# Fewer, larger weight transfers at the end of a decode kernel: A_wo in two transfers instead of four, B_w_down in four instead of five

## The chip, the cores and the metric

One core of one Trainium2 chip. The time is device microseconds (us) of a whole execution, the median of several; a fast run is one not slowed by a lower clock. The kernel before takes 81.61 us. The profile is one execution; its span, 79.8 us, is a little shorter than the timed execution.

In the profile, PE is the matrix engine (PEld its weight loads), DVE the vector engine, ACT the scalar engine, and SP the engine whose queue (SPq) issues the bulk transfers. A line of a timeline gives start and duration in us; `[0.49 <-DMA ...]` says that the engine had been idle for 0.49 us and that this transfer's landing ended the wait.

## The reference, cut to what matters

One token (512 values) goes through a layer norm, then through two branches that are added: attention with a window of 4096 cached keys and values (8 KV heads, 32 query heads of 128), closed by `@ wo`, and a gated MLP closed by `@ w_down`.

```
x  = A_x;  xn = layernorm(x)
a  = softmax(q @ k.T * 128**-0.5) @ v          # k, v: last 4096 rows of the caches, 8 heads
a  = a.reshape(1, 4096) @ wo                   # wo:     4096 x 512 bf16, 4.2 MB
y  = (silu(xn @ w_gate) * (xn @ w_up)) @ w_down   # w_down: 1792 x 512 bf16, 1.8 MB
out = x + a + xn + y * sigmoid(xn @ w_r)       # one token, so the routing picks it
```

With a single token every weight and every cached row is read once: 30.7 MB.

## The kernel before

All bulk loads are issued on the SP queue in the order in which they are used: wq, k, v, gate, up, wo, w_down. A_wo and w_down go to where the keys were, so their issue waits until the sixth head's keys have been copied away. In memory each of 128 partitions holds 32 consecutive rows of A_wo (32 KB) and 14 of w_down (14 KB). A transfer of 8 rows of A_wo is therefore 128 pieces of 8 KB.

```python
    def fill(n):                       # matmuls on zeros: keep TensorE's clock up
        for _ in range(2 * n):
            te.matmul(ps[:, 7, :], lhsT=zst[:], rhs=zmov[:], start=True, stop=True)
    # ... (scores, softmax, values, gate and up are cut) ...
    SP.need((s_c[1], 6))
    wo_v = A_wo.rearrange("(p j) n -> p (j n)", j=RJ)
    wo_chunks = [(0, 8), (8, 16), (16, 24), (24, 32)]
    t_wo = [dma(sy, f"wo{k}", wo_sb[:, j0 * D:j1 * D], wo_v[:, j0 * D:j1 * D]) for k, (j0, j1) in enumerate(wo_chunks)]
    wd_v = B_w_down.rearrange("(p j) n -> p (j n)", j=FB)
    wd_chunks = [(0, 4), (4, 8), (8, 11), (11, 13), (13, 14)]
    t_wd = [dma(sy, f"wd{k}", wd_sb[:, j0 * D:j1 * D], wd_v[:, j0 * D:j1 * D]) for k, (j0, j1) in enumerate(wd_chunks)]
    # ... cut ...
    for k, (j0, j1) in enumerate(wo_chunks):
        PE.need(t_wo[k])
        for j in range(j0, j1):
            ins = grouped(j, oT2[:, j:j + 1], wo_sb)      # one 1x512 matmul
        if k in (1, 2):
            with te.Fori(0, 3):
                fill(1)
    t_g4 = PE.mark(ins)
    DVE.need(t_g4, t_rf)
    fill(1)
    t_part = DVE.mark(ve.tensor_tensor(out=part, in0=a_ps, in1=rf, op=ALU.add))
    PE.need(t_hT)
    for k, (j0, j1) in enumerate(wd_chunks):
        PE.need(t_wd[k])
        for j in range(j0, j1):
            ins = by_halves(hTr[:, j, 0:1], wd_sb[:, j * D:(j + 1) * D], stop=(j == FB - 1))   # two 1x256 matmuls
        if k == 0:
            PE.need(t_part, t_sel4)
            by_halves(sel4[:], part)
    # ... two copies and the store of the result
```

Of the kernel before, what the change touches and what calls it, by code (L numbers as in the profile page):

```python
# [38 lines left out]
def kernel(  # L39
# [112 lines left out]
    te, ac, ve, gp, sy = nc.tensor, nc.scalar, nc.vector, nc.gpsimd, nc.sync  # L152

    def fill(n):
        for _ in range(2 * n):
            te.matmul(ps[:, 7, :], lhsT=zst[:], rhs=zmov[:], start=True, stop=True)  # L156

    def dma(eng, name, out_, in_):
        s = S("d_" + name)
        eng.dma_start(out=out_, in_=in_).then_inc(s, 16)  # L160
        return (s, 16)
# [192 lines left out]

    SP.need((s_c[1], 6))
    wo_v = A_wo.rearrange("(p j) n -> p (j n)", j=RJ)
    wo_chunks = [(0, 8), (8, 16), (16, 24), (24, 32)]
    t_wo = [dma(sy, f"wo{k}", wo_sb[:, j0 * D:j1 * D], wo_v[:, j0 * D:j1 * D]) for k, (j0, j1) in enumerate(wo_chunks)]
    wd_v = B_w_down.rearrange("(p j) n -> p (j n)", j=FB)
    wd_chunks = [(0, 4), (4, 8), (8, 11), (11, 13), (13, 14)]  # L360
    t_wd = [dma(sy, f"wd{k}", wd_sb[:, j0 * D:j1 * D], wd_v[:, j0 * D:j1 * D]) for k, (j0, j1) in enumerate(wd_chunks)]

    POOL.need((pe_t, 4 * HKV))
# [131 lines left out]
    def grouped(j, lhsT, w):  # L495
        c = j % 4
        return te.matmul(a_ps[32 * c:32 * c + 1, :], lhsT=lhsT, rhs=w[:, j * D:(j + 1) * D], start=False, stop=False,
                         tile_position=(0, 32 * c), skip_group_check=True)
# [7 lines left out]
    for k, (j0, j1) in enumerate(wo_chunks):  # L506
        PE.need(t_wo[k])
        for j in range(j0, j1):
            ins = grouped(j, oT2[:, j:j + 1], wo_sb)
        if k in (1, 2):  # L510
            with te.Fori(0, 3):
                fill(1)
    t_g4 = PE.mark(ins)
    DVE.need(t_g4, t_rf)
    fill(1)
    t_part = DVE.mark(ve.tensor_tensor(out=part, in0=a_ps, in1=rf, op=ALU.add))
    PE.need(t_hT)
    for k, (j0, j1) in enumerate(wd_chunks):
# [44 lines left out]
```

## Time and profile before

| | before |
|---|---|
| time, median of the first 3 runs | 81.61 us (81.58 to 81.94) |
| span of the profiled execution | 79.8 us |
| HBM read | 30.67 MB |
| last w_down transfer: middle part in / last part in | 75.31 / 76.82 us |

The DMA part of the page of before. Columns of the queue lines: packets, megabytes, and the time of their packets as a share of sixteen engines' span.

```profile
DMA packets 3178, 30.72 MB, mean 385 GB/s; under 512 B 356, under 2 KB 487, under 8 KB 999
...
q1 hardware_dynamic: 3170, 30.67, 91.9%
q8 instruction: 2, 0.03, 0.2%
q14 instruction: 2, 0.01, 0.0%
```

A packet is here one contiguous piece of one partition; the 356 smallest are mostly the writes to semaphores. The queues 8 and 14 are fetches of the program itself.

Two things that no view prints singly are used below: the trace's records of each packet (start, size, duration) and of each of the sixteen parts in which a transfer lands. Where they are quoted, it is as plain tables.

### The profile page before, as it was taken

How to read it: one execution, taken by the hardware profiler on the slowest of the kernel's cores; microseconds unless marked ns; L12 is line 12 of the kernel's file. 1: busy time of each engine (PE TensorE's matmuls, PEld its weight loads, DVE VectorE, ACT ScalarE, POOL GpSimd, SP SyncE). 2: the span in 40 equal slices, each digit the busy share in tenths (PEclk: the TensorE clock that was granted, in tenths of full speed). 3: DMA queues.
4: the chain of work that ended last, by engine and by line, in shares of the span. 5: the costliest groups of instructions: out<-in, count | busy, mean ns of one | idle time of the engine just before them, and what ended most of it. 6: DMA issues, size and time to landing. Idle time of an engine off the chain costs nothing.

```text
span 79.8 us, 1627 instructions
## 1 busy us (share of the span) xinstructions
PE 58.1 (73%) x634; PEld 30.3 (38%) x636; DVE 44.1 (55%) x96; ACT 30.4 (38%) x41; POOL 10.2 (13%) x22
## 2 busy tenths in 40 slices
PE   0010873849998997997996696778887799996750
PEld 0010401236875865865864224222232254231310
DVE  3778100166538769669693652988889348303020
ACT  1941000502379689589568026232233420000010
POOL 5930000000102202202205900000000000000000
PEclk9999999999999999999999999999999999999996
DMA  1899999999999999999999999999999999999600
GB/s 25 271 469 419 394 444 407 423 444 444 460 403 419 460 427 403 419 476 419 394 423 468 411 403 435 431 420 410 453 439 378 427 419 423 423 392 405 215 6 1
DMA packets 3178, 30.72 MB, mean 385 GB/s; under 512 B 356, under 2 KB 487, under 8 KB 999
## 3 DMA queue, kind: packets, MB, share of 16 engines
q1 hardware_dynamic: 3170, 30.67, 91.9%
q8 instruction: 2, 0.03, 0.2%
q14 instruction: 2, 0.01, 0.0%
q10 hardware_dynamic: 4, 0.00, 0.0%
HBM read 30.67 MB, written 0.00 MB: 385 GB/s over the span
## 4 chain that ended last, share of the span: by engine, by line
DMA 44%; SPq 22%; PE 18%; ACT 6%; DVE 4%; issue 2%
DMA k_sb<-in_B_w_down_dram 30%; SPq L160 22%; DMA wq_sb<-in_A_wq_dram 15%; PE ps L328 11%; ACT kT L303 6%; PE ps L337 3%; PE ps L256 2%; DVE kin L295 2%; PE ps L268 1%; DVE kT L300 1%; PE ps L502 1%; DVE qpad L273 1%; DVE kT L528 1%; SPq L558 0%; SPq L74 0%
## 5 line engine op out<-in xcount | busy, mean ns | idle before, releaser
L303 ACT COPY kT<-ps 128x1024 bf16<-128x1024 bf16 x19 | 18.6, 1015 | 9.6 <-PE ps L328 9.6
L328 PE MATMUL ps<-perm_bf,kin 128*128 128x128 bf16 x256 | 19.3, 235 | 1.2 <-DVE kin L295 0.9
L328 PEld LDWEIGHTS ps<-perm_bf,kin 128*128 128x128 bf16 x256 | 16.4, 106 | 5.7 <-issue 4.4
L295 DVE COPY kin<-k_sb 128x2048 bf16<-128x2048 bf16 x16 | 10.9, 686 | 3.1 <-PE ps L328 3.1
L300 DVE COPY kT<-ps 128x1024 bf16<-128x1024 bf16 x13 | 9.0, 691 | 4.1 <-PE ps L328 3.5
L423 ACT CAST pvS<-ps 128x512 bf16<-128x512 f32 x8 | 4.7, 585 | 10.0 <-PE ps L429 10.0
L337 PE MATMUL ps<-kT,qAB 128*32 128x512 bf16 x68 | 7.2, 414 | 1.7 <-ACT kT L303 1.7
L288 POOL COPY qAB<-qpad 128x64 bf16<-128x64 bf16 x8 | 3.5, 444 | 34.0 <-PE ps L337 34.0
L156 PE MATMUL ps<-zmov,zst 128*128 128x512 bf16 x25 | 6.6, 381 | 0.2 <-issue 0.2
L403 DVE COPY vin<-v_sb 128x2048 bf16<-128x2048 bf16 x8 | 5.5, 685 | 1.1 <-PE ps L438 0.9
L409 DVE COPY vin<-v_sb 128x2048 bf16<-128x2048 bf16 x8 | 5.5, 682 | 0.0
L438 PE MATMUL ps<-vin,pTcur 128*32 128x512 bf16 x32 | 3.2, 386 | 2.6 <-ACT pvS L423 2.2
L256 PE MATMUL ps<-wq_sb,xnT 128*1 128x512 bf16 x32 | 3.8, 621 | 1.7 <-DMA wq_sb<-in_A_wq_dram 1.7
L450 PE MATMUL ps<-zmov,zst 128*128 128x512 bf16 x16 | 4.7, 376 | 0.0
L529 ACT CAST kT<-ps 1x256 bf16<-1x256 f32 x1 | 0.4, 362 | 11.4 <-PE ps L502 11.4
L273 DVE COPY qpad<-ps 128x16 bf16<-128x16 bf16 x4 | 0.5, 170 | 7.5 <-PE ps L268 7.5
L212 PE MATMUL ps<-ident_bf,xn_row 1*128 1x1 bf16 x4 | 0.3, 166 | 4.8 <-POOL qAB L189 4.8
L262 ACT CAST q<-ps 128x512 bf16<-128x512 f32 x2 | 1.2, 585 | 6.6 <-PE ps L256 6.6
L444 PE MATMUL ps<-vin,pTcur 128*32 128x512 bf16 x32 | 3.2, 387 | 0.3 <-DVE vin L409 0.2
L337 PEld LDWEIGHTS ps<-kT,qAB 128*32 128x32 bf16 x68 | 1.9, 93 | 3.9 <-issue 1.7
L438 PEld LDWEIGHTS ps<-vin,pTcur 128*32 128x32 bf16 x32 | 1.1, 92 | 6.0 <-DVE vin L403 5.5
L156 PEld LDWEIGHTS ps<-zmov,zst 128*128 128x128 bf16 x26 | 2.0, 97 | 3.2 <-issue 1.7
(95 smaller groups left out, 54.2 us busy)
## 6 DMA issues: line engine op xcount, KB each, us to landing
v_sb<-in_A_v_cache_dram SPq DMA_DIRECT2D x4, 2048.0 KB, 39.7
k_sb<-in_A_k_cache_dram SPq DMA_DIRECT2D x3, 2048.0 KB, 24.1
wq_sb<-in_A_wq_dram SPq DMA_DIRECT2D x2, 2048.0 KB, 9.5
k_sb<-in_A_wo_dram SPq DMA_DIRECT2D x4, 1024.0 KB, 32.8
k_sb<-in_A_k_cache_dram SPq DMA_DIRECT2D x2, 1024.0 KB, 14.7
wq_sb<-in_B_w_gate_dram SPq DMA_DIRECT2D x1, 1792.0 KB, 42.9
wq_sb<-in_B_w_up_dram SPq DMA_DIRECT2D x1, 1792.0 KB, 46.9
k_sb<-in_B_w_down_dram SPq DMA_DIRECT2D x2, 512.0 KB, 33.8
```

Source lines behind the costliest of these rows:

```text
L156: te.matmul(ps[:, 7, :], lhsT=zst[:], rhs=zmov[:], start=True, stop=True)
L160: eng.dma_start(out=out_, in_=in_).then_inc(s, 16)
L256: ins = te.matmul(ps[32 * c:32 * c + 1, hf, :], lhsT=xnT[:, kt:kt + 1], rhs=wq_sb[:, kt, (4 * hf + c) * 512:(4 * hf + c + 1) * 512], start ...
L295: ve.tensor_copy(out=kin[:, 2 * h:2 * h + 2, :], in_=k_sb[:, g, 2 * h:2 * h + 2, :]).then_inc(s_c[h], 1)
L300: ve.tensor_copy(out=kT[:, b, :], in_=tp[:, b, :]).then_inc(s_ev[b], 1)
L303: ac.copy(out=kT[:, b, :], in_=tp[:, b, :]).then_inc(s_ev[b], 1)
L328: ins = te.transpose(tp[:, b, k * P:(k + 1) * P], kin[:, b, k * P:(k + 1) * P], perm_bf[:])
L337: ins = te.matmul(sc[32 * cq:32 * cq + 32, e, :], lhsT=qAB[:, e, :], rhs=kT[:, b, :].rearrange("d (k h q) -> d h k q", h=2, q=PH)[:, e], s ...
L403: ve.tensor_copy(out=vin[:, 0].rearrange("p (q k) d -> p q (k d)", q=4), in_=v_in[:, :, 0:4 * DH]).then_inc(s_va, 1)
L409: ve.tensor_copy(out=vin[:, 1].rearrange("p (q k) d -> p q (k d)", q=4), in_=v_in[:, :, 4 * DH:]).then_inc(s_vb, 1)
L423: ac.copy(out=pvS[:].rearrange("p t d -> p (t d)"), in_=pv_ps).then_inc(s_pvs, 1)
L450: te.matmul(ps[:, 7, :], lhsT=zst[:], rhs=zmov[:], start=True, stop=True)
```

## The change

Its intent: the stream of weights sets the end, so spend less of it on the fixed cost of a piece; and let fillers (matmuls on zeros, whose result nobody uses) cover the longer gap between the now larger arrivals.

```diff
-    wo_chunks = [(0, 8), (8, 16), (16, 24), (24, 32)]
+    wo_chunks = [(0, 16), (16, 32)]
...
-    wd_chunks = [(0, 4), (4, 8), (8, 11), (11, 13), (13, 14)]
+    wd_chunks = [(0, 7), (7, 11), (11, 13), (13, 14)]
...
-        if k in (1, 2):
-            with te.Fori(0, 3):
+        if k == 0:
+            with te.Fori(0, 8):
                 fill(1)
     t_g4 = PE.mark(ins)
     DVE.need(t_g4, t_rf)
-    fill(1)
+    fill(2)
```

## The prediction

> **What bounds the kernel now.** I read the page's forty slices first (is any unit full?), then the chain that ended last (which one sets the end?), then the last stretch of the chain in order of time, and last the timeline of the last 10 us, because the change sits there.
>
> The slices of the page, the DMA rows:
>
> ```profile
> PEclk9999999999999999999999999999999999999996
> DMA  1899999999999999999999999999999999999600
> GB/s 25 271 469 419 394 444 407 423 444 444 460 403 419 460 427 403 419 476 419 394 423 468 411 403 435 431 420 410 453 439 378 427 419 423 423 392 405 215 6 1
> ```
>
> Each slice is 2.0 us. The DMA engines are full from the second slice to about 75 us, at 380 to 470 GB/s, with no hole. The granted TensorE clock is full to the end of the work. No compute engine looks like that: PE is busy 73% of the span.
>
> The chain of waits from 50 us on, in order of time:
>
> ```profile
> 52.91 23.59 DMA k_sb<-in_B_w_down_dram
> 76.49 0.04 issue
> 76.54 0.61 PE ps L502 x6
> 77.15 0.02 issue
> 77.17 0.41 DVE kT L528
> ```
>
> The end is a landing of w_down at 76.5 us, then a handful of matmuls, a copy and the store. Before that the chain follows the queue itself. So the kernel is one stream of 30.7 MB and what follows its last byte.
>
> How fast the stream is by size of piece, from stretches in which one size dominates (22 to 50 us: 16 KB pieces; 60.2 to 70 us: A_wo in 8 KB pieces); the last columns are DMA share and GB/s:
>
> ```profile
> 22.00:50.00 28.00, 24.48 (x315) 16.58 (x312) 18.55 (x31) 19.16 (x22) 6.18 (x10) 1.00 1.01 427
> ...
> 60.20:70.00 9.80, 8.66 (x100) 3.47 (x104) 5.52 (x13) 1.89 (x4) 0.00 (x0) 1.00 1.01 422
> ```
>
> The timeline of the tail, PE and DVE:
>
> ```profile
> 67.33 1.03 PE L497 MATMUL ps<-k_sb,oT 128*1 128x512 bf16 x16
> ...
> 68.30 1.47 PE L156 MATMUL ps<-zmov,zst 128*128 128x512 bf16 x6
> ...
> 69.88 0.60 PE L497 MATMUL ps<-k_sb,oT 128*1 128x512 bf16 x8
> ...
> 72.37 0.60 PE L497 MATMUL ps<-k_sb,oT 128*1 128x512 bf16 x8 [0.49 <-DMA k_sb<-in_A_wo_dram]
> ...
> 73.03 0.69 DVE L516 TENSOR_TENSOR kT<-ps,kT 128x512 f32<-128x512 f32 x1 [4.48 <-PE ps L497]
> ...
> 74.93 0.60 PE L502 MATMUL ps<-k_sb,hTr 128*1 128x256 bf16 x8 [0.16 <-DMA k_sb<-in_B_w_down_dram]
> 75.88 0.49 PE L502 MATMUL ps<-k_sb,hTr 128*1 128x256 bf16 x6 [0.34 <-DMA k_sb<-in_B_w_down_dram]
> 76.54 0.60 PE L502 MATMUL ps<-k_sb,hTr 128*1 128x256 bf16 x6 [0.16 <-DMA k_sb<-in_B_w_down_dram]
> ```
>
> From 68 us on every batch of useful matmuls starts when its chunk lands; between them PE runs fillers (L156). PE has room here, the stream has none.
>
> The landing records add one thing. Each transfer lands in 16 parts. Up to 40 us all 16 come within 0.4 us; from then on one part, and from 52 us two parts, come late: the last w_down transfer has 14 parts in by 75.45 us, then 76.15 and 76.82. The end therefore hangs on one DMA engine that is 1.5 us behind the middle one.
>
> **What the Trainium skill says.**
> "DMA: Bandwidth & Descriptors", section Rules for kernel authors, asks for 128 partitions and at least 1 MiB per DMA. A_wo has that already (four of 1 MiB), and the trace's 422 against 427 GB/s says little is left to win by size.
> The same page, in the section on why a DMA increments its semaphore by 16, says the sixteen engines finish independently and only the full 16 means that all has landed. The trace agrees: a wait ends with the latest engine (76.82 us, middle 75.31 us).
> "Runtime: NRT & Kernel Launch", Instruction fetch mechanics: instructions are refilled in 16 KiB blocks of 256 through a DMA queue. The trace shows it: queue 8 of kind "instruction" has 2 packets, 0.03 MB, at 47.5 and 74.8 us, each over 1 us long. The first falls just before the second engine becomes late.
> "TensorE: Matmul & The Clock Gate", Part 1, describes a clock that falls to half after an idle window of about 3.4 us. That is what the fillers are for; with them the trace shows a granted clock of 1.00 through the tail.
>
> **The change part by part.**
>
> A_wo: 32 rows per partition, four transfers of 8 rows (8 KB pieces) become two of 16 rows (16 KB pieces). Bytes are the same. The trace's packet records (start, size, duration of each; no view prints them singly) give after 40 us a mean of 313.5 ns for 8 KB and 617.7 ns for 16 KB. Each of 16 DMA engines serves 8 of the 128 partitions: before 4 x 8 x 313.5 = 10.03 us, after 2 x 8 x 617.7 = 9.88 us. Gain 0.15 us. Cross-check by the windows: 4.19 MB at 422 against 427 GB/s is 9.94 against 9.82 us, 0.12 us.
>
> w_down: pieces of 4, 4, 3, 2, 1 KB become 7, 4, 2, 1 KB. Means: 4 KB 162.6, 3 KB 124.4, 2 KB 86.2, 1 KB 46.5 ns; 7 KB, a line between 4 and 8 KB, 275.8 ns. Per engine before 8 x (162.6 + 162.6 + 124.4 + 86.2 + 46.5) = 4.66 us, after 8 x (275.8 + 162.6 + 86.2 + 46.5) = 4.57 us. Gain 0.09 us.
>
> Three transfers fewer: three semaphore writes of 9.4 ns per engine, 0.03 us.
>
> All of this lies on the stream that sets the end, so it counts in full: 0.15 + 0.09 + 0.03 = 0.27 us. The last transfers stay 2 KB and 1 KB pieces, so the work after the last landing (76.82 to the end of the span, 2.95 us) does not change.
>
> PE before the tail: the first A_wo batch. Before, the second chunk had landed at 67.34 us, just as its matmuls began; after, one chunk of 16 rows lands at about 67.2 us, and the sixteen matmuls start at 67.33 us as before. Nothing gained or lost. Then fillers: before 2 loops of 3 (12 matmuls), after one of 8 (16). Six fillers took 1.47 us, so a further one costs about (1.47 - 0.38) / 5 = 0.22 us; sixteen are 0.38 + 15 x 0.22 = 3.7 us, 68.3 to 72.0 us. The second half lands at 72.33 - 0.15 = 72.2 us. The loop fits, with 0.2 us to spare.
>
> PE after it: sixteen matmuls at once instead of eight, 1.03 instead of 0.60 us: 72.2 to 73.2 us, where before it was 72.97. The addition on DVE (0.69 us) ends at about 74.0 instead of 73.7 us. Two pairs of fillers instead of one cover that gap. The first w_down chunk has seven rows and lands near 74.4 us: the landing of eight rows (74.89) less one row (8 x 46.5 ns, at most 0.37) and less the 0.2 us gained by then, so 74.3 to 74.5. It meets a finished addition. Fourteen matmuls at about 0.05 us apart are issued by 75.1 us, the four of the addition's row sum (0.35 us) by 75.5, and the next chunk lands at 75.84 - 0.2 = 75.6 us. PE is caught up, with 0.1 to 0.2 us of slack, and once more before the last two chunks (76.2 and 76.55 us). None of it reaches the end.
>
> Sum: 81.61 - 0.27 = 81.34 us.
>
> **The rivals.**
>
> PE becomes the bound in the tail: bigger first chunks leave more matmuls after a landing. For it: 16 instead of 8 matmuls after A_wo's last landing, 14 instead of 8 after w_down's first. Against it: the waits of 0.16 to 0.49 us before each later batch, and the slack above. If I mis-sized a batch by 0.3 us it would still be made good before 76.5 us. A loss of 0.2 us in all at most: 81.5 us.
>
> The late DMA engine moves. Its delay of 1.5 us is worth more than the whole change. For it: instruction blocks are fetched over the same engines, and the change shortens PE's program in the tail (one loop out, two matmuls in), so that the fetch at 74.8 us may come a little elsewhere. If it fell on the late engine while that still had data, the end would come 0.6 us later (one 16 KB packet): 81.9 us. Against it: the fetch at 47.5 us is upstream of every edit, the shift of the other is a few instructions and to later ones, and now it leaves the late parts' distance unchanged (1.60 us at the first w_down chunk, 1.51 at the last). The other way, if a delay fell on a second engine instead, 0.7 us would be won: 80.6 us.
>
> Size doesn't matter at all: the gain is below what two runs differ by (81.58 to 81.94). Then 81.6 us. Against it: the packet durations differ cleanly between sizes, by more than their scatter, though by 1.5% only.
>
> Clock: one longer loop of fillers could leave a gap elsewhere. With no idle stretch over 1 us foreseen, I give it nothing.
>
> **Range and chances.** The mean of these is near 81.35 us. Scatter of a median of few runs is about 0.15 us, the PE rival gives +0.2, the late engine -0.7 to +0.6 with perhaps one chance in ten. That makes 81.0 to 81.75 us for 8 in 10. To be faster by over 2% it would have to be under 79.98 us, 1.6 us away: more than the late engine's whole delay. Slower by over 2% is over 83.24 us, for which I see no path. So 0.02, 0.96, 0.02.
>
> **What would show it.** Right: the landing of A_wo's second half about 0.15 us before 72.3 us, of the last w_down chunk about 0.27 us before 76.82; total packets 3170 - 384 - 48 = 2738 on queue 1; waits for w_down still ending every later L502 batch; the same two late parts, 0.8 and 1.5 us behind. Wrong: an L502 batch released by the DVE addition or running without a wait into the next (PE bound); the late parts at another distance (then the time moves with them, whatever the sizes do); a mean 16 KB packet of A_wo that is not near 618 ns, or a granted clock below 1.00 before 77 us.

## The result

The changed kernel took 81.44 us (81.18 to 81.52, 6 runs) against 81.61 us (81.54 to 81.94, 6 runs). The ratio is 0.997, 95% interval 0.9949 to 0.9992. A ratio here is the mean time of one kernel's fast runs over that of the other's of the same rounds, so it isn't quite the ratio of the medians. Of 81.61 us, 0.3% is 0.24 us.

The DMA part of the page of the changed kernel:

```profile
DMA packets 2745, 30.72 MB, mean 386 GB/s; under 512 B 307, under 2 KB 438, under 8 KB 822
...
q1 hardware_dynamic: 2738, 30.67, 91.8%
q8 instruction: 2, 0.03, 0.2%
```

432 packets fewer on queue 1 for the same bytes: exactly the 384 pieces and 48 semaphore writes that the prediction counted.

The same two stretches of the changed kernel; the last columns are again DMA share and GB/s:

```profile
22.00:50.00 28.00, 22.76 (x290) 14.58 (x291) 19.70 (x36) 16.93 (x21) 5.61 (x9) 1.00 1.01 427
60.20:70.00 9.80, 7.31 (x84) 3.17 (x85) 3.42 (x9) 1.13 (x2) 0.00 (x0) 1.00 1.01 428
```

The first stretch, which the change doesn't touch, reads 427 GB/s as before. The second, A_wo, went from 422 to 428.

The timeline of the tail after, PE:

```profile
67.49 1.03 PE L497 MATMUL ps<-k_sb,oT 128*1 128x512 bf16 x16 [2.19 <-DMA k_sb<-in_A_wo_dram]
68.45 3.63 PE L156 MATMUL ps<-zmov,zst 128*128 128x512 bf16 x16
72.29 1.03 PE L497 MATMUL ps<-k_sb,oT 128*1 128x512 bf16 x16 [0.21 <-DMA k_sb<-in_A_wo_dram]
73.26 1.04 PE L156 MATMUL ps<-zmov,zst 128*128 128x512 bf16 x4
74.57 0.93 PE L502 MATMUL ps<-k_sb,hTr 128*1 128x256 bf16 x14 [0.27 <-DMA k_sb<-in_B_w_down_dram]
75.33 0.60 PE L502 MATMUL ps<-kT,sel 128*1 128x256 f32 x4
75.76 1.22 PE L502 MATMUL ps<-k_sb,hTr 128*1 128x256 bf16 x14
```

and DVE:

```profile
73.38 0.69 DVE L516 TENSOR_TENSOR kT<-ps,kT 128x512 f32<-128x512 f32 x1 [6.94 <-PE ps L497]
77.02 0.41 DVE L528 CAST kT<-ps 1x256 bf16<-1x256 f32 x1 [2.95 <-PE ps L502]
```

Each batch still begins at a landing. The sixteen fillers fit between the halves of A_wo with 0.2 us to spare. The addition is done at 74.07 us, half a microsecond before the first w_down batch can start. The last batch is written as one row of fourteen, but it waits inside: fourteen matmuls take 0.93 us when nothing holds them, and 1.22 us here. By the trace's records its three parts start at 75.76, 76.38 and 76.70 us, each 0.04 to 0.07 us after its transfer's last part (75.69, 76.34, 76.66).

The chain of waits of the changed kernel from 50 us on, in order of time:

```profile
33.93 40.50 DMA k_sb<-in_B_w_down_dram
74.43 0.14 issue
74.57 1.80 PE ps L502 x26
76.36 0.02 issue
76.38 0.61 PE ps L502 x6
77.00 0.02 issue
77.02 0.41 DVE kT L528
```

At first sight this chain reads as if PE had taken over at 74.57 us: 26 matmuls in a row for 1.80 us. That is the view merging batches whose idle time is short. The wait table of the tail tells it:

```profile
PEld ps L502 <- DMA k_sb<-in_B_w_down_dram: 0.9, 3, 0.3
PEld ps L502 <- DVE kT L516: 0.7, 1, 0.7
PE ps L502 <- DMA k_sb<-in_B_w_down_dram: 0.3, 1, 0.3
```

Three later w_down batches waited for their transfer by up to 0.3 us each (before: 2.0 us in four waits). The 0.7 us put down to DVE is the first batch's weight load, which the addition did not hold up: it was done at 74.07, and the batch started at 74.53, 0.1 us after its transfer's last part (74.43). The slack shrank; the bound did not change.

One more thing differs, and doesn't matter: in this trace the scores ran about 2 us earlier than in the trace of before (PE waits 2.19 us for the first half of A_wo). The stream isn't affected: in the two repeats of the same kernel this wait is 1.03 and 0.84 us, and the middle of the last transfer lands at the same time (table of the repeats below).

### The profile page after: what moved, and what is told of

It is laid out like the page before. It is cut to its first block, busy times and chain, and to the rows that moved or that the text cites. A ratio compares the mean times of both kernels' runs of the same rounds, so it can differ in the third digit from the quotient of the medians.

```text
span 79.6 us, 1641 instructions
## 1 busy us (share of the span) xinstructions
PE 55.3 (69%) x642; PEld 28.8 (36%) x642; DVE 43.6 (55%) x96; ACT 30.3 (38%) x41; POOL 10.2 (13%) x22
## 4 chain that ended last, share of the span: by engine, by line
DMA 76%; PE 9%; ACT 4%; SPq 4%; DVE 3%; issue 1%
DMA k_sb<-in_B_w_down_dram 51%; DMA k_sb<-in_A_k_cache_dram 25%; PE ps L328 5%; ACT kT L303 4%; SPq L160 4%; PE ps L502 3%; DVE kin L295 2%; PE ps L337 1%; DVE kT L300 1%; DVE kT L528 1%; SPq L558 0%; SPq L74 0%
## 5 line engine op out<-in xcount | busy, mean ns | idle before, releaser
L328 PE MATMUL ps<-perm_bf,kin 128*128 128x128 bf16 x256 | 17.1, 220 | 2.4 <-DVE kin L295 2.1
L328 PEld LDWEIGHTS ps<-perm_bf,kin 128*128 128x128 bf16 x256 | 14.3, 98 | 6.4 <-issue 3.6
L156 PE MATMUL ps<-zmov,zst 128*128 128x512 bf16 x32 | 7.9, 381 | 0.0
L450 PE MATMUL ps<-zmov,zst 128*128 128x512 bf16 x16 | 4.7, 376 | 0.0
L516 DVE TENSOR_TENSOR kT<-ps,kT 128x512 f32<-128x512 f32 x1 | 0.7, 692 | 6.9 <-PE ps L497 6.9
L156 PEld LDWEIGHTS ps<-zmov,zst 128*128 128x128 bf16 x32 | 2.7, 98 | 3.7 <-issue 1.3
L256 PE MATMUL ps<-wq_sb,xnT 128*1 128x512 bf16 x32 | 2.9, 499 | 1.6 <-DMA wq_sb<-in_A_wq_dram 1.6
L497 PE MATMUL ps<-k_sb,oT 128*1 128x512 bf16 x32 | 2.1, 378 | 2.4 <-DMA k_sb<-in_A_wo_dram 2.4
## 6 DMA issues: line engine op xcount, KB each, us to landing
wq_sb<-in_B_w_up_dram SPq DMA_DIRECT2D x1, 1792.0 KB, 47.7
```

The costliest lines, as they stand in the source:

```text
L328: ins = te.transpose(tp[:, b, k * P:(k + 1) * P], kin[:, b, k * P:(k + 1) * P], perm_bf[:])
```

## The experiments

Every verdict below is against the kernel before in the same rounds, on one chip per group. Groups ran on different chips.

### A_wo alone

```diff
-    wd_chunks = [(0, 7), (7, 11), (11, 13), (13, 14)]      # rest as in the changed kernel
+    wd_chunks = [(0, 4), (4, 8), (8, 11), (11, 13), (13, 14)]
```

> A_wo alone in two 16 KB-piece transfers with the long loop of fillers; w_down in its five old transfers. Theory (every packet has a fixed cost, the stream sets the end): 16 packets and 2 semaphore writes fewer per DMA engine, 0.17 us less than before: 81.44 us, ratio 0.998; the middle part of the last w_down transfer lands at about 75.14 us instead of 75.31. Rival (the gain came from the longer filler loop or from scatter): 81.6 us with the middle landing unmoved, or the whole 0.2 to 0.25 us of the changed kernel.

Measured: 81.28 against 81.68 us, ratio 0.9947 (0.9931 to 0.9963): 0.39 us by the means. The middle part of the last transfer landed at 75.13 us, as expected to 0.01 us. So the stream behaved as the packets say, but the time fell by twice as much, more even than the changed kernel's. That called for a repeat (below).

### w_down alone

```diff
-    wd_chunks = [(0, 4), (4, 8), (8, 11), (11, 13), (13, 14)]      # rest as before
+    wd_chunks = [(0, 7), (7, 11), (11, 13), (13, 14)]
```

> w_down alone in four transfers; A_wo and its fillers as before. Theory: 8 packets and one semaphore write fewer per engine, 0.10 us less: 81.51 us, ratio 0.9988, the middle part of the last transfer at about 75.22 us. Rival (gain only from A_wo or scatter): 81.6 us, middle landing unmoved at 75.31 us.

Measured: 81.58 against 81.68 us, ratio 0.9982 (0.9966 to 0.9999), 0.16 us by the means; middle landing 75.23 us. Both lie near 0.10 us. One landing time of one trace does not settle it, though: kernels that have all transfers of the changed kernel show the last middle landing anywhere from 74.99 to 75.22 us. A measure with less scatter follows the table of the repeats.

### The opposite direction, in a large dose

```diff
-    wo_chunks = [(0, 8), (8, 16), (16, 24), (24, 32)]
+    wo_chunks = [(j, j + 4) for j in range(0, 32, 4)]
-    wd_chunks = [(0, 4), (4, 8), (8, 11), (11, 13), (13, 14)]
+    wd_chunks = [(j, j + 1) for j in range(14)]
-        if k in (1, 2):          # fillers after the same rows as before
+        if k in (3, 5):
-        if k == 0:               # row sum after the same rows as before
+        if k == 3:
```

> The opposite direction in a dose that clears the noise: A_wo in eight transfers of 4 KB pieces, w_down in fourteen of 1 KB pieces, the fillers of before at the same rows. Theory: per engine A_wo 64 x 162.6 ns instead of 32 x 313.5 and w_down 112 x 46.5 ns instead of 4.66 us, 13 more semaphore writes: +0.41 +0.64 = +1.05 us, 82.65 us, ratio 1.013; middle landing of the last part near 76.35 us. Rival (size of pieces does not matter, the late engine's distance and scatter do): 81.6 us plus or minus 0.3.

Measured: 82.39 against 81.68 us, ratio 1.0084 (1.007 to 1.0098), 0.71 us. The sign and order are right and the rival is out: smaller transfers of smaller pieces cost time by themselves. In the profiled execution the middle part landed at 76.27 us, 0.96 us later than before, near the expected 1.05; but the six timed runs show only 0.71. Their spans average 80.6 us and those of before in the same rounds 79.9, so the profiled pair (80.7 and, from earlier, 79.8) lies at the two far ends. So the one trace shows nine tenths of the expected dose and the runs two thirds of it; the landings of the other runs are not on record, and why the rest is missing is open. The page shows how many pieces there were:

```profile
DMA packets 5049, 30.72 MB, mean 381 GB/s; under 512 B 563, under 2 KB 2358, under 8 KB 3382
```

The mean durations of packets after 60 us, from the records of these traces, with what a byte costs:

```
piece     ns      ns per KB   from the trace of
 1 KB     46.5      46.5      before (50.0 in the fine pieces, 53.6 in the last experiment)
 2 KB     86.2      43.1      before
 3 KB    124.4      41.5      before
 4 KB    162.6      40.6      before
 7 KB    275.2      39.3      changed
 8 KB    313.5      39.2      before
16 KB    614.6      38.4      changed
32 KB   1217.1      38.0      A_wo in one (below)
```

A piece costs about 37.5 ns per KB and 9 to 17 ns more. From 8 to 32 KB there are 3% to win in all; 1 KB pieces cost a quarter more than 37.5 ns per KB.

Two limits of this price. A record's duration is not quite what a piece takes from the stream: the fourteen 1 KB transfers of the fine pieces land 0.374 us apart (middle parts, 71.03 to 76.27 us), which is 46.8 ns for a piece with its share of the semaphore write, and their records say 50.0 ns, so neighbouring records overlap. And nearly every transfer has 128 pieces, so the size of a piece and of a transfer go together. A cost per transfer beyond the semaphore write has no room, though: A_wo's transfers of before land 2.48 to 2.50 us apart, and eight pieces of 313.5 ns with one semaphore write already make 2.52 us.

### A_wo in a single transfer

```diff
-    wo_chunks = [(0, 16), (16, 32)]         # rest as in the changed kernel
+    wo_chunks = [(0, 32)]
...
-        if k == 0:
-            with te.Fori(0, 8):
-                fill(1)
...
+    with te.Fori(0, 10):                    # ahead of all A_wo matmuls
+        fill(1)
```

> As the changed kernel, but A_wo in a single transfer of 32 KB pieces; the loop of fillers, ten long, stands before all 32 matmuls. Theory (stream sets the end, PE has slack): packets of 32 KB would save another 0.1 us per engine: 81.25 to 81.35 us, and every later batch of w_down still waits for its landing. Rival (PE becomes the bound when the batch after the landing doubles): 32 matmuls from 72.2 us, the addition only at about 74.0 to 74.7 us, w_down batches then run without waits and the end comes at least 0.3 us after the changed kernel's: 81.75 us or more.

Measured: 81.44 against 81.68 us, ratio 0.9978 (0.9962 to 0.9995): 0.19 us under before, no better than the changed kernel. The tail in its timeline:

```profile
71.98 1.90 PE L497 MATMUL ps<-k_sb,oT 128*1 128x512 bf16 x32 [0.93 <-DMA k_sb<-in_A_wo_dram]
...
73.81 1.04 PE L156 MATMUL ps<-zmov,zst 128*128 128x512 bf16 x4
73.93 0.69 DVE L515 TENSOR_TENSOR kT<-ps,kT 128x512 f32<-128x512 f32 x1 [6.05 <-PE ps L497]
...
74.78 0.93 PE L502 MATMUL ps<-k_sb,hTr 128*1 128x256 bf16 x14
75.54 0.60 PE L502 MATMUL ps<-kT,sel 128*1 128x256 f32 x4
...
75.97 0.93 PE L502 MATMUL ps<-k_sb,hTr 128*1 128x256 bf16 x14
```

Here PE is the bound: the 32 matmuls and the four fillers behind them last until 74.85 us, the first w_down batch starts 0.6 us after its transfer was in (74.14 us), and the last fourteen matmuls run in 0.93 us without a wait. The last transfer was in at 76.37 us, and the result copy starts 0.58 us later, at 76.95, where before and the changed kernel need 0.35 us. The theory's 0.1 us is there in the packets (1217 ns against 2 x 614.6, eight times), and PE gives it back. The four fillers have a share in this that the experiment did not separate: they run from 73.81 to 74.85 us, while the first w_down transfer was in at 74.14 us. A version without them was not run; whether 32 matmuls behind one landing would delay the end by themselves is open. The expectation that each w_down batch would still wait for its landing was wrong; the rival's loss of 0.3 us was too large by time, but right in kind. So, with these fillers, the changed kernel stops one step short of where PE takes over.

### The changed kernel and A_wo alone again

The same files, unedited.

> The changed kernel again, unedited, for its scatter against the A_wo-only version (81.28 us, ratio 0.9947) and the first measurement (81.44 us, ratio 0.9970). If the parts add, it should be the faster of the two, ratio near 0.993. If only the packets count, 0.27 us less than before: 0.9967. If one measurement of this size just has that scatter, something between 0.994 and 0.998.

> The changed kernel once more, as the reference for the other two in the same rounds: by the packets 0.27 us under before, ratio 0.9967; by the two measurements so far between 0.18 and 0.25 us under it.

> A_wo alone again, beside the changed kernel in the same rounds. If packets are all: 0.17 us under before, 0.10 us over the changed kernel. If the first measurement (0.43 us under before) was more than scatter: again 0.35 us or more under before, and not slower than the changed kernel.

Measured, by the means of the same rounds:

| version | by packets | ratio (95%) | us under before | middle / last part of the last transfer |
|---|---|---|---|---|
| changed, first | -0.27 | 0.9970 (0.9949 to 0.9992) | 0.24 | 75.05 / 76.66 |
| changed, second | -0.27 | 0.9978 (0.9945 to 1.0011) | 0.18 | 75.04 / 76.61 |
| changed, third | -0.27 | 0.9954 (0.9935 to 0.9973) | 0.41 | 75.10 / 76.44 |
| A_wo alone, first | -0.17 | 0.9947 (0.9931 to 0.9963) | 0.39 | 75.13 / 76.67 |
| A_wo alone, second | -0.17 | 0.9987 (0.9960 to 1.0014) | 0.17 | 75.14 / 76.51 |
| w_down alone | -0.10 | 0.9982 (0.9966 to 0.9999) | 0.16 | 75.23 / 76.72 |

The second group has one run of 82.12 us among six, the last group one of 81.97 in A_wo alone; they are kept. Repeats of the same file differ by over 0.2 us between groups, so a single group can't tell A_wo alone from the whole change. The means are 0.28 us for the changed kernel and 0.28 us for A_wo alone; in the one group that ran both, the changed kernel was 0.24 us faster. The middle landings follow the packets within 0.06 us in all six rows.

They do so better when the start of the stream is taken out: count from the middle landing of the up weights (near 60.8 us), the last transfer that no version edits, to that of the last w_down transfer:

```
version                          us from up to the end of w_down   by packets
before                           14.52
w_down alone                     14.46                             -0.10
A_wo alone                       14.36, 14.35 (repeat)             -0.17
changed                          14.28, 14.28, 14.28 (repeats)     -0.27
same transfers, other edits:
  much shorter PE program        14.27                             -0.27
  shorter PE, padded programs    14.29, 14.29                      -0.27
  count of engines               14.33                             -0.27
A_wo in one                      14.21                             -0.37
fine pieces                      15.50                             +1.05
```

Repeats of one file agree within 0.02 us here. In the stream the change is worth 0.24 us of the 0.27, A_wo alone 0.16 to 0.17 of 0.17, and w_down 0.06 to 0.07 of 0.10: both parts add, and the price by packets is a little too high.

### Is the late engine late because of the program's own fetches?

The last part of the last transfer comes 1.3 to 1.6 us after the middle one, and the end waits for it: nearly 2% of the time, many times the change. The prediction pointed at a fetch of instructions just ahead of the second late part and left it at that. Three edits of the changed kernel test it.

```diff
# shorter program for PE (wrong result: one of four terms of gate and up)
-        for kt in range(KT):
+        for kt in range(1):
# much shorter (wrong result): that, and half of the q and of the A_wo matmuls left out
# padded DVE and ACT programs (correct result), ahead of the scores
+    for i in range(12):
+        ve.memset(junk[:, 4 + i:5 + i], 0.0)
+    for i in range(12):
+        ac.copy(out=junk[:, 18 + i:19 + i], in_=eps_t[0:1, :])
```

> Wrong result on purpose: 24 of the 32 gate and up matmuls left out, which shortens PE's program by 48 instructions to about 500 and frees PE time far from the bound. Theory (the block of 16 KB instructions fetched near 46 to 49 us makes one DMA engine late by about 1.5 us, and the end waits for it): with less than 512 instructions the third block is not needed, its fetch and that late part go, the last landing comes 0.6 to 1.5 us earlier: 79.9 to 80.8 us. Rival 1 (the fetch comes when the 256th instruction is passed, whatever the length): it stays where it is, the late parts too, 81.4 us. Rival 2 (the late parts have nothing to do with fetches): late parts unchanged even if the fetch is gone.

Measured: 81.39 against 81.62 us, ratio 0.9965 (0.9951 to 0.9978), the same as the changed kernel. Both fetches of queue 8 were still there, at 47.7 and 75.5 us, and the late parts too (middle 75.22, last 76.66 us). My theory of the program's length fell. Rival 1 fits what was seen; rival 2 is not tested, since no fetch went away.

> Wrong result on purpose: half of the q and A_wo matmuls left out as well, PE's program about 110 instructions shorter. Theory (fetch at passing a block boundary): the first fetch moves from 46-49 us to well after, near 60 us, or goes, and the second late part appears only after it. Rival (late parts unrelated): the second late part still appears between 47 and 52 us.

Measured: 81.32 us in one run. Queue 8 fetched once, at 48.1 us; the second fetch was gone. The second late part appeared after the first fetch, as before, and the last part came at 76.58 us (middle 75.11). So the fetch near 75 us contributes nothing to the lateness, and the one near 47 us stayed, at a time within the range of the other traces (46.3 to 48.7 us) and not near 60 us. The expectation was wrong there. By the count of matmuls the fetch did move: it came when 383 had started, as in all other traces (383 to 389), though 16 q matmuls ahead of it had been left out. So it moved later in PE's program by about as many, which fits a block boundary, but not clearly in time.

> Twelve tiny memsets added on DVE and twelve tiny copies on ACT ahead of the scores, to see whose program the 8 KB fetch near 38 to 40 us (queue 14) belongs to; DVE runs about 6 and ACT about 4 instructions in each 3 us there. If DVE's: the fetch and the first late part come about 6 us earlier; if ACT's, about 9 us earlier; if neither's, unmoved. If the late part is unrelated to the fetch, it stays at the transfer that lands at 42.4 us in any case. Time unchanged within 0.3 us.

Measured: 81.21 us in one run, correct. The 8 KB fetch of queue 14 came at 32.7 us instead of 37.8 to 40.3 us, some 6 us earlier, as foreseen if it is DVE's (9 us if ACT's). The counts of the trace lean the same way: DVE had started 63 of the instructions in the trace when the fetch came (59 to 61 in the other traces), ACT 36 (29 or 30). Both programs were padded in one run, so this is likely and not shown. And the first late part now showed up one transfer earlier: at the v transfer whose middle part lands at 37.4 us, one part came at 38.44 us, where all other traces have all sixteen in by 37.92 us. So an edit that moved the fetch moved the late part with it. This is one trace of one run, and the trace doesn't say which DMA engine carries the fetch. It is the strongest evidence here that the fetch causes the lateness. The amount isn't explained: the 8 KB fetch takes 0.33 us by its record and the part comes 0.6 to 1.3 us late.

For the 16 KB fetch of queue 8 no edit moved it far, but its time varies by itself between 46.3 and 48.7 us, while the third v transfer's middle part always lands at 47.2 to 47.4 us. In the six traces with the fetch at 46.97 us or earlier, that transfer already has two late parts; in the eight with the fetch at 47.36 us or later, it has one, and the next transfer has two. All fourteen traces sort that way:

```
fetch (us)  parts late in the third v transfer     trace of
46.34       2 (48.41, 48.97)                       changed
46.77       2 (48.26, 48.93)                       padded
46.84       2 (48.15, 49.00)                       engine count
46.87       2 (48.34, 49.03)                       w_down alone
46.92       2 (48.01, 49.08)                       changed, second
46.97       2 (48.26, 49.13)                       fine pieces
47.36       1 (48.37)                              A_wo in one
47.37       1 (48.33)                              changed, third
47.49       1 (48.27)                              before
47.54       1 (48.34)                              last row on fewer engines
47.73       1 (48.34)                              shorter PE
47.97       1 (48.34)                              A_wo alone, second
48.13       1 (48.12)                              much shorter PE
48.72       1 (48.20)                              A_wo alone
```

It is a correlation, without an edit, but one without an exception.

### Which engines are late

```diff
+    probe = sb("probe", [P, 15 * 128], BF16)
...
+    t_pr = [dma(sy, f"pr{n}", probe[0:n, (n - 1) * P:n * P], A_wo[0:n, 0:P]) for n in range(15, 0, -1)]   # behind w_down
...
-    POOL.need(t_out)
+    POOL.need(t_out, *t_pr)
```

> A measurement, on the changed kernel: fifteen small transfers of 15, 14, ... 1 partitions (256 B each) queued behind the last w_down transfer, each split over as many DMA engines as it has partitions, so that the arrivals of one and the next name the engine that is in the one and not in the other. Theory (a fetch of instructions goes to one fixed engine per program): exactly two of the sixteen are late, by about 0.7 and 1.5 us, and the arrivals tell which; the transfer that leaves out the latest lands 0.7 to 1.5 us before the ones that have it. Rival (the lateness is of one partition's addresses or of the transfer, not of an engine): the small transfers land together, or the late parts do not follow the number of engines. The result is correct; the time may be up to 0.5 us longer.

Measured: correct, 81.36 us. The two latest arrivals of each of the small transfers (us):

```
partitions   second latest   latest
   15           76.03         76.74
   14           76.21         76.91
   13           76.38         77.08
   12           76.57         77.27
   11           76.19         76.76   <- the latest is gone, the second now leads
   10           76.40         76.94
  ...
    5           76.97         77.84
    4           77.11         78.03
    3           77.26         77.28   <- the second late one is gone too
```

That a transfer of n partitions is split over n engines is seen in the trace: each has n arrivals beside one entry at the start. Each step adds 0.17 to 0.19 us to both series, since it brings one more small piece. The latest engine's series 76.74, 76.91, 77.08, 77.27 stops between 12 and 11 partitions; the other late one's series 76.03, 76.21, 76.38, 76.57, 76.76, 76.94 and so on to 78.03 stops between 4 and 3. The Trainium skill ("DMA: Bandwidth & Descriptors", Why a DMA increments its semaphore by 16 and not by 1) says that a transfer issued on this path, from SP, takes the lowest-numbered k engines. If so, the late ones are engine 11 and engine 3. The counts agree with such an order, since the late engines left the transfers singly, at 12 to 11 and at 4 to 3 partitions; the numbers themselves stand in no trace. The lateness belongs to engines, whatever the transfer.

### A version meant to beat both

```diff
+    # last row of w_down: 121 partitions on engines 0 to 10, 7 partitions on engines 0 to 6
+    j0, j1 = wd_chunks[-1]
+    t_wd.append([dma(sy, f"wdl{p0}", wd_sb[p0:p1, j0 * D:j1 * D], wd_v[p0:p1, j0 * D:j1 * D]) for p0, p1 in ((121, P), (0, 121))])
```

(The other chunks are as in the changed kernel; the last batch waits for both transfers.)

> A version meant to beat both: the changed kernel with the last w_down row (1 KB pieces) sent as a transfer of 121 and one of 7 partitions, which run on DMA engines 0 to 10 and 0 to 6, so that the latest engine, number 11, has nothing to do in it. Theory (the end waits for engine 11, 1.5 us late; engine 3 is 0.7 us late): engine 11 is done with the row before (76.34 us in the changed kernel), engine 3 takes 12 pieces instead of 8, 75.80 + 12 x 0.046 + 0.1 for the extra transfer = 76.45 us, so the last landing comes 0.2 us before 76.66: 81.2 us, 0.2 us under the changed kernel in the same rounds. Rival (engine 11 isn't what the end waits for, or small transfers cost more than they save): no gain or up to 0.3 us slower than the changed kernel.

Measured: 81.68 against 81.69 us, ratio 1.0026 (0.9992 to 1.0059), and 0.5 us slower than the changed kernel in the same rounds. It failed. The row was split as meant: its two transfers have 11 and 7 arrivals beside the entry at the start, and only one late part each. It was in at 76.35 us, near the expected 76.45. But the transfer ahead of it, which still uses engine 11, came in at 76.51 us, where the changed kernel's was in at 76.34 (76.12 in the same rounds): in this trace the latest engine fell back against the middle one from 1.69 to 1.93 us between the first and the second w_down transfer, the other late one with it. And now six matmuls follow the latest landing instead of two:

```profile
75.97 1.08 PE L504 MATMUL ps<-k_sb,hTr 128*1 128x256 bf16 x14
...
77.09 0.36 ACT L531 CAST kT<-ps 1x256 bf16<-1x256 f32 x1 [11.30 <-PE ps L504]
```

The copy starts at 77.09 us, 0.58 us after the landing at 76.51, against 0.36 us after it in the changed kernel. My estimate had left that batch out. Why the late engines fell back isn't known. And the trace is of the fastest of the six runs (81.44 us); for the others, up to 82.37 us, there is no trace, so part of the 0.5 us stays unexplained. So no version here is shown to beat the changed kernel.

## Why the prediction was right, and where not

The predicted 81.35 us and the range hold; the gain by the means is 0.24 us in the first measurement and 0.28 us over three, against 0.27. That the times come so close is in part luck, since single groups gave 0.18 to 0.41 us; the stream's own 0.24 us, with its scatter of 0.02, is the better test.

- The bound. Right: the stream sets the end, before and after; every direct test of a piece's size moved the middle landing as its packets say (table above).
- The sum. 16 KB pieces took 614.6 ns (617.7 reckoned), 7 KB pieces 275.2 (275.8), and the packets fell by the 432 counted. The middle part of the last transfer came 0.26 us earlier, of 0.27 (0.24 counted from the up weights). What follows the last landing took 2.95 us in both traces, as foreseen.
- The last part came only 0.16 us earlier in the first trace (76.66 instead of 76.82, 0.27 foreseen), because the late engine was 1.60 instead of 1.50 us behind. The prediction expected that distance to stay. It does not: 1.28 to 1.60 us over the traces, and in the changed kernel's first trace it was 1.68 already at the gate and up weights, which no edit touches, so the change has no part in it. That is also why A_wo's first half came at 67.35 and not 67.2 us; besides, the 67.2 took off the whole saving of A_wo where only half had been gained, 0.08 us.
- PE. The first sixteen matmuls began at 67.49 us, not 67.33, behind that landing. The fillers took 3.63 us (3.7), the addition ended at 74.07 (74.0), the first w_down transfer came at 74.43 (74.3 to 74.5), and w_down's later batches each waited. The slack of 0.1 to 0.2 us was small indeed: A_wo in one transfer, with the fillers behind it, used it up. The chain and the wait table of the changed kernel show what the prediction gave as a sign of being wrong (a w_down batch put down to the DVE addition, batches run together); the landings show that it was the views' reading and not PE. The clock, to which the prediction gave nothing, was granted in full: 1.00 from 60 to 77 us.
- The rival of the moving fetch. The fetch at 75 us has no effect that shows (much shorter program, one run). The prediction called the one at 47 us safe because it lies upstream of every edit; it does move by itself, between 46.3 and 48.7 us, and its lateness stays.
- The scatter. I took 0.15 us for a median of few runs. Groups of the same file differed by 0.23 us by their means (0.18 to 0.41 us under before), so the range was not too wide.
- The readings. Two were loose: the second slice has 271 GB/s and one slice 476, outside the "380 to 470", and the landing "at 76.5 us" of the chain is that of the last transfer but one; the end hangs on 76.82 us, as the prediction says further down.

## What to carry to other kernels

When one full stream of transfers sets the end, a change of piece size can be priced from the trace alone: count the pieces each engine handles, multiply by the measured duration of a piece of that size, and compare. In the stream the price came out a tenth too high for the whole change (0.24 of 0.27 us) and a third too high for w_down (0.06 to 0.07 of 0.10); in time the fine pieces cost 0.71 us of 1.05. Merge until the consumer has just slack enough: one more step (A_wo in one) saved 0.07 us in the stream and lost it again at PE, behind four fillers that stood in the way. Look at the landing of all sixteen parts before counting gigabytes: here one engine late by 1.5 us is worth more than five times the change, and sending the last row around it did not help: in its trace the transfer ahead of that row came later, and more work followed the last landing.

## What the Trainium skill lacked or had wrong

- "DMA: Bandwidth & Descriptors" has its measured table by size of a whole transfer, for the other issuing path, and its rule asks for 1 MiB per DMA. It gives no duration for a contiguous piece of several KB on the path from SP. In the full queue here a piece took 162.6 ns for 4 KB, 313.5 for 8 KB, 614.6 for 16 KB, 1217 for 32 KB. Going from 1 MiB to 2 MiB transfers gained 0.15 us of 10.
- "Runtime: NRT & Kernel Launch", Instruction fetch mechanics, calls the cost of crossing a block mostly hidden. For the engine that executes it may be; for a saturated stream it seems not to be: after an 8 KB fetch one DMA engine was 0.6 to 1.3 us behind the middle one, after a 16 KB fetch another one 1.3 to 1.9 us, to the end of the kernel. That the fetches cause it rests on one edited trace and the sorting of fourteen. No page speaks of such a delay of the data.
- The same section speaks of 16 KiB blocks. PE's fetches were 16 KB; the one that moved when DVE's and ACT's programs were padded, DVE's by its shift, was 8 KB.
